# The gate's weights times `w_out`: summed on VectorE instead of multiplied on TensorE

## The chip, the cores and the metric

One NeuronCore of a Trainium2 chip. The metric is the device time of one launch in microseconds (us), as a median of runs. Engines are named as in the profile: PE is TensorE (matmuls; PEld are its weight loads), DVE is VectorE, ACT is ScalarE, POOL is GpSimd, SP is the engine whose queue issues most DMAs.

## What is computed

Sparse attention (4 batches, 8 heads, 576 positions, 64 wide), a gated mixture without routing, and a mixture of 8 experts with a greedy routing. Cut to what matters here:

```
x = attention(q, k, v)                   # 2304 tokens x 512
h = (x @ w1) * (x @ w2) @ w3             # 512 -> 1024 -> 1024
y = h @ w_out                            # 2304 x 512
logits = y @ w_gate                      # 2304 x 8
order = argsort(-logits)                 # greedy: each token one expert, 288 tokens per expert
out[mask_e] = relu(y[mask_e] @ e1[e]) @ e2[e]
```

`w_out` is 1024x512, `w_gate` 512x8, `w3` 1024x1024.

## The kernel before

The kernel never multiplies by `w3`, `w_out` and `w_gate` one after the other. It makes the product g = (x @ w1) * (x @ w2) for all tokens, and beside it two small weights: W = w3 @ w_out for the tokens' rows, and WG = w3 @ w_out @ w_gate for the logits, so that the routing can start from g @ WG at once.

Main products are exact to fp32 by splits: each operand is written as a high part h (rounded by ACT) and a rest l = x - h, and a product is h h + h l + l h (three fp32r matmuls). A split of a 128x1024 weight tile (`split`, L118 to L125) is one copy on ACT (L121) and one subtraction (L124): a single one of 1024 columns on DVE, or four of 256 columns on POOL where it is given `nc.gpsimd`.

The order of each engine's instructions is the order in which the Python program emits them. The mixture (`moe`, L445) is a generator that is run once for each batch b. For each f of 8 (128 columns of the 1024) it computes a = x @ w1 and b = x @ w2 into PSUM tiles of tag "ab" (four banks, used in turn), copies a to SBUF on ACT (L482) and multiplies it by b on DVE (L484: `g<-a,ps_ab`, or `gt<-a,ps_ab` for the 256-wide part). It yields before each step of matmuls: the 512-wide part has four steps of six matmuls for each f, the 256-wide part (b = 3 alone, the last 64 tokens of each batch together) two steps of twelve. The copy and the multiplication of a step are emitted at the yield behind it. The loop over batches puts other work between the steps: attention of later batches while b < 3, and for b = 3 the generator `gates` (L378), one piece a step.

`gates` makes WG. Before, in b = 3, from the fourth step on: eight turns, in which PE transposes four 128x128 blocks of `w_out` (L390, fetched as fp32 into the tiles `wo`) into PSUM, ACT copies them (L392, `wt`), and PE multiplies them by the gate's weights, padded to 32 columns (L398). The result is copied, transposed back (L411) and stands as the tile TS: for each of the 1024 rows of `w_out` its 8 products. Then TS times `w3` in two groups of 64 matmuls (L421), with six steps between them in which the second half of `w3` is loaded (`fetch_w3`), and two transposes (L433) give WG. Loads come from a DRAM scratch `kept`, on SP's queue. From the third f of the 512-wide part on, `place3` (L364) splits one pair of tiles of `w_out` and `w3` for the later product W, its subtraction on POOL.

The tile pools `p2` and `p3` (for `wo`, `wt`, `S`) take the room of the attention's pool `pa`, so their loads wait for attention's last instructions.

Of the kernel before, what the change touches and what calls it, by code (L numbers as in the profile page):

```python
# [32 lines left out]
C_I40, C_I96, C_PC = 136, 256, 352  # L33
C_PR, C_RS, C_M8, C_END = 460, 468, 612, 620

START, ATT_RATE, RUSH, LATE, EARLY, FIRST, ALONE = 8, 0.65, 0.65, 3, 7, 0.7, 18

ONE, GATHER_F = 2, 1

# [48 lines left out]
def body(tc, qk_d, v_d, ke_d, ve_d, msk_d, cst_d, tri_d, w1_d, w2_d, w3_d, wo_d, wg_d, e1_d, e2_d, out):  # L88
# [26 lines left out]
    def wtile(tag):  # L115

        return [wp.tile([128, 1024], F32R, tag=tag, name=tag + n, bufs=8) for n in "hl"]
# [243 lines left out]
        nc.sync.dma_start(t, kept[x])  # L361
        narrowed[x] = t

    def place3():  # L364
        n, i = to_split[placed[0]]
        k, tag = (2, "wa") if n == "wo" else (8, "wb")
        pre[n, i] = [x.rearrange("p (k n) -> p k n", k=k) for x in split(narrowed.pop((n, i)), *wtile(tag), nc.gpsimd)]
        placed[0] += 1
        if n == "w3" and i >= 2 and i + 2 < 8:
            fetch(("w3", i + 2), pm.tile([128, 1024], F32, tag="f", name="f", bufs=2))  # L370
# [4 lines left out]
    TS = TS[:, 256:].rearrange("p (m e) -> p m e", m=8)  # L375

    def gates():
        wg32 = p3.tile([128, 4, 32], F32, name="wg32", bufs=1)  # L378
        dve.memset(wg32, 0.0)
        dve.tensor_copy(wg32[:, :, 0:8], wg)  # L380
        dve.memset(TS, 0.0)
        acc = bank([128, 2, 128], "rt")

        def turn(r):
            g, i = divmod(r, 4)
            t = bank([128, 4, 128], "h")
            for q in range(4):
                w = narrowed["wo", 2 * g + q // 2]
                n0 = 512 * (q % 2) + 128 * i
                nc.tensor.transpose(t[:, q, :], w[:, n0:n0 + 128], ident)  # L390
            wt = p3.tile([128, 4, 128], F32, tag="wt", name="wt", bufs=2)
            act(wt, t, AF.Copy)  # L392
            return wt

        def gate(r, wt):
            g, i = divmod(r, 4)
            for q in range(4):
                mm(acc[32 * q:32 * q + 32, g, :], wg32[:, i, :], wt[:, q, :], start=(i == 0), stop=(i == 3))  # L398

        for r in range(0, 8, 2):  # L400
            wts = [turn(r), turn(r + 1)]
            yield
            yield
            for i in range(2):
                gate(r + i, wts[i])
        ts = p3.tile([128, 4, 128], F32, tag="wt", name="ts", bufs=2)[:, :2]
        act(ts, acc, AF.Copy)
        yield
        t = bank([128, 2, 128], "tr")
        for g in range(2):  # L410
            nc.tensor.transpose(t[:, g, :], ts[:, g, :], ident)  # L411
        dve.tensor_copy(TS.rearrange("p (g q) e -> p g q e", g=2)[:, :, :, 0:8],
                        t.rearrange("p g (q e) -> p g q e", q=4)[:, :, :, 0:8])
        yield

        acc = bank([128, 2, 128], "rt")
        for a, ms in enumerate(((4, 5, 6, 7), (0, 1, 2, 3))):
            ws = [narrowed["w3", m] for m in ms]
            for k in range(8):
                for q, w in enumerate(ws):  # L420
                    mm(acc[32 * q:32 * q + 32, a, :], TS[:, k, :], w[:, 128 * k:128 * k + 128],  # L421
                       start=(k == 0), stop=(k == 7))
            yield
            if ms[0]:
                fetch_w3(0)
                for _ in range(6):
                    yield
        wt = p3.tile([128, 4, 128], F32, tag="wt", name="wt", bufs=2)[:, :2]
        act(wt, acc, AF.Copy)
        yield  # L430
        t = bank([128, 2, 128], "tr")
        for a in range(2):
            nc.tensor.transpose(t[:, a, :], wt[:, a, :], ident)  # L433
        for a in range(2):
            dve.tensor_copy(WG[:, 4 - 4 * a:8 - 4 * a, :], t[:, a, :].rearrange("p (q e) -> p q e", q=4))

    def fetch_w3(m):
        x = p3.tile([128, 2, 1024], F32, tag="S", name="S", bufs=1)
# [7 lines left out]
    def moe(b):  # L446

        full = [(f, 2) for f in range(CUT[b] if b < 3 else 0, 8)]
        if b < 3:
            todo = [(f, h) for h in range(2) for f in range(CUT[b])] + full  # L450
        else:
            todo = [(f, 3) for f in range(8)] + full
        late = []
        for f, part in todo:
            if part == 3:
                xh, xl = XT
                if not GT:
                    GT.append(slot(0, [128, 8, 64 * B], F32, "gt"))
                ts, out = slice(0, 64 * B), GT[0][:, f]
            else:  # L460
                xh, xl = X[b]
                if b not in G:
                    G[b] = [slot(((4, 5), (6, 7), (8, 9), (1, 10))[b][i], [128, 4, MAIN], F32, "g") for i in range(2)]
                ts = (slice(0, HEAD), slice(HEAD, MAIN), slice(0, MAIN))[part]
                out = G[b][f // 4][:, f % 4, ts]
            nt = ts.stop - ts.start
            for n in (1, 2):
                for k in range(4):
                    if k == 0 or k == 2 and part == 2:
                        yield part, f, n  # L470
                        while late:
                            late.pop()()
                    if k == 0:
                        a = bank([128, nt], "ab")
                        wh, wl = W[n, f // 2]
                        fs = slice((f % 2) * 128, (f % 2) * 128 + 128)
                    mm(a, wh[:, k, fs], xh[:, k, ts], start=(k == 0), stop=False)  # L477
                    mm(a, wh[:, k, fs], xl[:, k, ts], start=False, stop=False)  # L478
                    mm(a, wl[:, k, fs], xh[:, k, ts], start=False, stop=(k == 3))  # L479
                if n == 1:  # L480
                    a_sb = pm.tile([128, MAIN], F32, tag="a", name="a", bufs=1)[:, :nt]
                    late.append(lambda x=a_sb, a=a: act(x, a, AF.Copy))  # L482
                else:
                    late.append(lambda x=a_sb, a=a, out=out: dve.tensor_tensor(out, x, a, op=OP.mult))  # L484
        while late:
            late.pop()()
# [21 lines left out]
        GS[c] = h, l  # L508


    wg = cst.tile([128, 4, 8], F32, name="wg")
    att = attention()
    qk_load(0)
# [17 lines left out]
            next(narrow, None)  # L531

    for b in range(B):
        if b == 3:
            stacks.pop("pa").close()
            p2 = pool("p2")
            p3 = pool("p3")
            for i in range(2):
                x = p2.tile([128, 2, 1024], F32, tag=f"P{i}", name="wo", bufs=1)
                for n in range(2):  # L540
                    fetch(("wo", 2 * i + n), x[:, n])
            fetch_w3(4)
            making_wg = gates()
        if b == 2:
            for _ in narrow:
                pass
        steps = 0
        for done, (part, f, n) in enumerate(moe(b)):
            if b == 0:
                while (n, f // 2) not in W:  # L550
                    next(narrow, None)
            while b < 3 and nxt is not None and nxt < NB * (b + 2) and (
                    steps < done * (RUSH if b == 0 else ATT_RATE) + (min(done, 8) * FIRST if b == 0 else 0) or nxt < NB * b + (8 if part else 4)):
                nxt = next(att, None)
                steps += 1
            if b < 2:
                next(narrow, None)
            if b == 3:
                if done >= LATE:
                    next(making_wg, None)  # L560
                while part == 2 and placed[0] // 2 < f // 2:
                    place3()
        while nxt is not None and nxt < NB * (b + 1) + (8 if b < 2 else 9):
            nxt = next(att, None)
    for _ in making_wg:
        pass
    while placed[0] < 8:
        place3()
# [14 lines left out]
    def make_w():  # L583

        for m in range(8):
            a = bank([128, D], "ab")
            for k in range(8):
                while ("wo", k // 2) not in pre or ("w3", m) not in pre:
                    place3()
                h, l = pre["w3", m]  # L590
                oh, ol = pre["wo", k // 2]
                mm(a, h[:, k, :], oh[:, k % 2, :], start=(k == 0), stop=False)
                mm(a, h[:, k, :], ol[:, k % 2, :], start=False, stop=False)
                mm(a, l[:, k, :], oh[:, k % 2, :], start=False, stop=(k == 7))
                yield 680
            evac(m, a)
            if placed[0] < 12:
                place3()
            if m in (4, 5):
                gsplit(m - 4)  # L600
        est.extend(pm.tile([128, 1024], F32, tag="f", name="est", bufs=2) for _ in range(2))
# [620 lines left out]
```

## Time and profile before

| | |
|---|---|
| median of 3 runs | 724.92 us (723.85 to 726.5) |
| the profiled execution | 727.11 us |
| its span, first to last instruction | 725.3 us |
| PE busy | 701.6 us, 97% of the span |
| DVE busy | 410.7 us, 57% |
| ACT busy | 353.2 us, 49% |
| POOL busy | 265.7 us, 37% |
| mean granted clock of PE | 0.978 of full speed |

Attention and the first three batches of the mixture fill about the first 223 us of the span, the last batch 223 to 301, then come the logits, W, the rows for the experts beside the routing, and the experts. Busy shares are means over stages with different limits. Matmuls are pipelined, so a row's duration is longer than the distance to the next row; it is the distance that counts.

### The profile page before, as it was taken

Reading aid. Unit: us, or ns where it says so; the run is one execution under the profiler, and the core shown is the slowest. Engines: PE = TensorE matmul, PEld = TensorE weight load, DVE = VectorE, ACT = ScalarE, POOL = GpSimd, SP = SyncE. Lnnn points to the kernel's source line nnn. Section 1 sums busy time; section 2 is a strip of 40 time slices with the busy share of each in tenths; the row PEclk is TensorE's granted clock in tenths of the full one; section 3 lists DMA queues with packets and bytes.
Section 4 is the critical chain, followed back from the end, with each engine's and each line's share of the span. In section 5 each row is a group of like instructions: output and inputs, shape, how many; then the busy total and the mean of one; then the engine's idle time right before and its main releaser. Section 6 shows DMA issues by size and latency. Waiting matters only on the chain.

```text
span 725.3 us, 15966 instructions
## 1 busy us (share of the span) xinstructions
PE 701.6 (97%) x6081; PEld 611.1 (84%) x6081; DVE 410.7 (57%) x1414; ACT 353.2 (49%) x812; POOL 265.7 (37%) x305
## 2 busy tenths in 40 slices
PE   4799999999999999999999999999999999999996
PEld 3689778888889988687877777799999999999995
DVE  5879867684312111167886768778888763234321
ACT  6666544454522222243445375447575656655432
POOL 2848512231100024533365353331414236655421
PEclk9589999999999999999999999999999999999998
DMA  8994687872105120110699999969988898996311
GB/s 302 340 280 165 219 331 271 298 271 104 52 5 228 39 79 1 60 35 31 117 131 136 169 137 232 155 205 225 248 239 244 197 277 226 299 288 188 93 33 33
DMA packets 59596, 126.66 MB, mean 175 GB/s; under 512 B 13696, under 2 KB 29440, under 8 KB 56960
## 3 DMA queue, kind: packets, MB, share of 16 engines
q1 hardware_dynamic: 27232, 89.46, 36.1%
q0 software_dynamic: 29696, 31.46, 26.3%
q10 hardware_dynamic: 2592, 4.72, 1.9%
q8 instruction: 48, 0.79, 0.4%
q14 instruction: 28, 0.23, 0.1%
HBM read 87.87 MB, written 15.73 MB: 143 GB/s over the span
## 4 chain that ended last, share of the span: by engine, by line
PE 84%; issue 6%; DVE 3%; POOL 2%; DMA 2%; ACT 1%; POOLq 0%; SPq 0%; ACTq 0%
PE ps_ab L477 10%; PE ps_ab L478 9%; PE ps_ab L479 9%; PE ps_ab L623 5%; PE ps_ab L625 4%; PE ps_ab L624 4%; PE ps_h L1047 4%; PE ps_h L1048 3%; PE ps_h L1049 3%; PE ps_ab L1071 3%; PE ps_ab L1072 3%; PE ps_ab L1073 3%; PE ps_rt L822 3%; PE ps_rt L228 2%; DMA qk<-qk_dram 2%
## 5 line engine op out<-in xcount | busy, mean ns | idle before, releaser
L207 POOL TENSOR_TENSOR p<-p,sm 128x384 f32<-128x384 f32 x36 | 45.8, 1283 | 123.0 <-DVE sm L205 75.4
L1071 PE MATMUL ps_ab<-hh,w 128*128 128x288 f32 x248 | 76.2, 307 | 0.0
L1073 PE MATMUL ps_ab<-hh,w 128*128 128x288 f32 x248 | 73.1, 295 | 0.0
L1072 PE MATMUL ps_ab<-hl,w 128*128 128x288 f32 x248 | 73.0, 294 | 0.0
L507 POOL DMA_DIRECT2D wbl<-g x36 | 48.4, 1675 | 61.1 <-ACT wbl L505 52.0
L1060 DVE SCALAR_TENSOR_TENSOR hl<-ps_h,hh 128x288 fp32r<-128x288 f32 x62 | 28.2, 455 | 70.3 <-ACT hh L1059 70.1
L1059 ACT ACTIVATE hh<-ps_h 128x288 fp32r<-128x288 f32 x62 | 25.5, 412 | 84.0 <-PE ps_h L1049 81.3
L200 ACT ACTIVATE p<-p,sm 128x96 f32<-128x96 f32 x144 | 52.0, 363 | 25.2 <-DVE sm L193 24.3
L482 ACT ACTIVATE a<-ps_ab 128x512 f32<-128x512 f32 (+1 forms) x44 | 22.9, 522 | 81.4 <-PE ps_ab L479 73.0
L623 PE MATMUL ps_ab<-Wx,wbh 128*128 128x512 f32 x144 | 59.6, 414 | 0.0
L625 PE MATMUL ps_ab<-Wx,wbl 128*128 128x512 f32 x144 | 56.2, 391 | 0.0
L477 PE MATMUL ps_ab<-x,wah 128*128 128x512 f32 (+1 forms) x144 | 55.5, 386 | 0.7 <-ACT x L251 0.7
L624 PE MATMUL ps_ab<-Wx,wbh 128*128 128x512 f32 x144 | 56.2, 390 | 0.0
L477 PE MATMUL ps_ab<-x,wbh 128*128 128x512 f32 (+1 forms) x144 | 54.5, 379 | 0.0
L478 PE MATMUL ps_ab<-x,wah 128*128 128x512 f32 (+1 forms) x144 | 54.0, 375 | 0.0
L479 PE MATMUL ps_ab<-x,wal 128*128 128x512 f32 (+1 forms) x144 | 53.7, 373 | 0.0
L479 PE MATMUL ps_ab<-x,wbl 128*128 128x512 f32 (+1 forms) x144 | 53.3, 370 | 0.0
L478 PE MATMUL ps_ab<-x,wbh 128*128 128x512 f32 (+1 forms) x144 | 53.2, 370 | 0.0
L484 DVE TENSOR_TENSOR g<-a,ps_ab 128x512 f32<-128x512 f32 (+1 forms) x36 | 22.5, 624 | 54.0 <-PE ps_ab L479 51.1
L1072 PEld LDWEIGHTS ps_ab<-hl,w 128*128 128x128 f32 x248 | 46.7, 188 | 0.1
L1071 PEld LDWEIGHTS ps_ab<-hh,w 128*128 128x128 f32 x248 | 46.7, 188 | 0.0
L1073 PEld LDWEIGHTS ps_ab<-hh,w 128*128 128x128 f32 x248 | 46.5, 188 | 0.0
(296 smaller groups left out, 2044.3 us busy)
## 6 DMA issues: line engine op xcount, KB each, us to landing
est<-e_dram SPq DMA_DIRECT2D x53, 512.0 KB, 5.9
w<-w_dram SPq DMA_DIRECT2D x16, 1024.0 KB, 8.0
qk<-qk_dram SPq DMA_DIRECT2D x36, 320.0 KB, 4.7
w<-est POOLq DMA_DIRECT2D x20, 512.0 KB, 7.8
wbl<-g POOLq DMA_DIRECT2D x28, 256.0 KB, 6.5
v<-v_dram SPq DMA_DIRECT2D x36, 192.0 KB, 4.4
kept<-f SPq DMA_DIRECT2D x12, 512.0 KB, 4.1
rows<-e_dram SPq DMA_DIRECT2D x11, 512.0 KB, 5.8
```

Source lines behind the costliest of these rows:

```text
L200: act(p[:, i, :], p[:, i, :], AF.Exp, bias=sm[:, 1, i:i + 1], scale=-1.0, accum_out=sm[:, 2, i:i + 1])
L207: nc.gpsimd.tensor_tensor(p, p, sm[:, 3, :, None].to_broadcast([128, 4, KB]), op=OP.mult)
L477: mm(a, wh[:, k, fs], xh[:, k, ts], start=(k == 0), stop=False)
L478: mm(a, wh[:, k, fs], xl[:, k, ts], start=False, stop=False)
L479: mm(a, wl[:, k, fs], xh[:, k, ts], start=False, stop=(k == 3))
L507: nc.gpsimd.dma_start(x, src, accum_op=OP.add)
L623: mm(a, h[:, f, :], wh, start=(f == 0), stop=False)
L624: mm(a, h[:, f, :], wl, start=False, stop=False)
L625: mm(a, l[:, f, :], wh, start=False, stop=(f == 7))
L1071: mm(y, wh[:, f % 2, ds_], h, start=(f == 0), stop=False)
L1072: mm(y, wh[:, f % 2, ds_], l, start=False, stop=False)
L1073: mm(y, wl[:, f % 2, ds_], h, start=False, stop=(f == end))
```

## The change

TS is no longer made by PE. The gate's weights (128 x 32) are transposed once on PE (L380 of the changed kernel), copied by ACT (`ws`) and written to DRAM as `wgt`, 32 rows of 128. For each of the 8 experts SP reads its 512 weights back, replicated over all 128 partitions (`wt`, two buffers). DVE then multiplies each of the eight 128x512 blocks of `w_out` by that row and sums along the row, one column of TS an instruction (L400): 64 instructions, two a mixture step, all with the same unused full output `waste`. The generator starts as soon as attention's last instructions are emitted, within b = 2, and is stepped within `moe`, behind the late copies and products. The `w3` loads stand behind `wgt` and the first two rows. Splits start when WG is done; those up to the eighth are now on DVE, the others stay on POOL.

```
-    def place3():
+    def place3(eng=None):
...
-        pre[n, i] = [x.rearrange("p (k n) -> p k n", k=k) for x in split(narrowed.pop((n, i)), *wtile(tag), nc.gpsimd)]
+        pre[n, i] = [x.rearrange("p (k n) -> p k n", k=k) for x in split(narrowed.pop((n, i)), *wtile(tag), eng)]
...
     def gates():
...
-        for r in range(0, 8, 2):
-            wts = [turn(r), turn(r + 1)]
+
+        t = bank([32, 128], "h")
+        nc.tensor.transpose(t, wg.rearrange("p c e -> p (c e)"), ident)
+        ws = p3.tile([32, 128], F32, name="ws", bufs=1)
+        act(ws, t, AF.Copy)
+        wgt = dram.tile([32, 128], F32, name="wgt")
+        nc.sync.dma_start(wgt, ws)
         dve.memset(TS, 0.0)
+        waste = p3.tile([128, 512], F32, name="waste", bufs=1)
+
+        def row(e):
+            w = p3.tile([128, 4, 128], F32, tag="wt", name="wt", bufs=2)
+            nc.sync.dma_start(w, wgt.rearrange("(c e) p -> e c p", c=4)[e:e + 1].to_broadcast([128, 4, 128]))
+            return w.rearrange("p c n -> p (c n)")
+
+        rows = [row(e) for e in range(2)]
+        fetch_w3(4)
+        for _ in range(3):
             yield
+        for e in range(8):
+            w = rows.pop(0)
+            for m in range(8):
+                dve.tensor_tensor_reduce(waste, narrowed["wo", m // 2][:, 512 * (m % 2):512 * (m % 2) + 512], w, scale=1.0,
+                                         scalar=0.0, op0=OP.mult, op1=OP.add, accum_out=TS[:, m, e:e + 1])
+                if m % 2:
+                    yield
+            if e < 6:
+                rows.append(row(e + 2))
...
                         while late:
                             late.pop()()
+                        for x in side:
+                            next(x, None)
...
+            if b == 2 and nxt is not None and nxt >= NT:
+                nxt = None
+                stacks.pop("pa").close()
...
+                side.append(gates())
             if b == 3:
-                if done >= LATE:
-                    next(making_wg, None)
-                while part == 2 and placed[0] // 2 < f // 2:
+                if gated and part == 2 and placed[0] < 6:
                     place3()
...
-                    place3()
+                    place3(nc.gpsimd)
```

How the order moves. On PE in the 256-wide part of b = 3, before, a gate product and the next transposes stand between two steps of the mixture:

```order
L479 MATMUL ps_ab<-xt,wal 128x256
L398 MATMUL ps_rt<-wt,wg_2891 32x128 x8
L390 MATMUL ps_h<-C,wo 128x128 x8
L477 MATMUL ps_ab<-xt,wbh 128x256
L478 MATMUL ps_ab<-xt,wbh 128x256
```

In the changed kernel nothing stands there, and the first group of TS times `w3` (now L412) comes in the 512-wide part, half way through the second product of its fourth f:

```order
L471 MATMUL ps_ab<-x,wbh 128x512
L472 MATMUL ps_ab<-x,wbh 128x512
L473 MATMUL ps_ab<-x,wbl 128x512
L412 MATMUL ps_rt<-S,TS 32x128 x2
L412 MATMUL ps_rt<-f,TS 32x128 x2
```

That group reads TS, so PE's queue stands there until DVE has made all of TS. On DVE at the end of b = 2 and the start of b = 3, before, with the semaphores that each row waits for in brackets:

```order
L484 TENSOR_TENSOR g<-a,ps_ab 128x512 [waits PE_49]
L484 TENSOR_TENSOR g<-a,ps_ab 128x512 [waits PE_49,Activation_49]
L484 TENSOR_TENSOR gt<-a,ps_ab 128x256 [waits PE_49,Activation_49]
L379 MEMSET wg_2891 128x128 [waits DMAHW4_49,DMAHW3_49,DMAHW5_49,DMAHW2_49,DMAHW6_49,DMAHW1_49,DMAHW7_49,DMAHW0_49,Pool_49]
L380 COPY wg_2891<-wg 128x4x8 [waits DVE_49]
```

And in the changed kernel, where a sum is two rows, the sum itself and the read of its accumulator into TS:

```order
L478 TENSOR_TENSOR g<-a,ps_ab 128x512 [waits PE_49]
L385 MEMSET TS 128x256
L400 ISA waste,TS<-wo,wt 128x512 [waits DMAHW3_49,DMAHW4_49,DMAHW2_49,DMAHW5_49,DMAHW1_49,DMAHW6_49,DMAHW0_49,DMAHW7_49,DVE_49,Pool_49]
L400 ISA TS 128x1
L400 ISA waste,TS<-wo,wt 128x512 [waits DVE_49]
L400 ISA TS 128x1
L478 TENSOR_TENSOR g<-a,ps_ab 128x512 [waits PE_49,Activation_49]
L400 ISA waste,TS<-wo,wt 128x512 [waits DMAHW6_49,DVE_49]
L400 ISA TS 128x1
L400 ISA waste,TS<-wo,wt 128x512 [waits DVE_49]
```

The last product of b = 2 now stands behind the first two sums, and each sum carries a wait for DVE's own semaphore, DVE_49. On SP, behind the loads of `wo`, before:

```order
L361 DMA wo<-kept 128x1024 x3
L361 DMA S<-kept 128x1024 x2
L361 DMA f<-kept 128x1024 x2
```

and in the changed kernel:

```order
L361 DMA wo<-kept 128x1024 x3
L384 DMA wgt<-ws 32x128 [waits Activation_49]
L390 DMA wt<-wgt 128x4x128 [waits DMAHW1_49]
L390 DMA wt<-wgt 128x4x128
L361 DMA S<-kept 128x1024
```

The read of the first row waits for a DMA's semaphore, and the loads of `w3` (into `S` and `f`) stand behind it.

## Rows read from the trace of the kernel before

**Rows 1.** The page, part 1: busy us (share of the span) xinstructions.

```profile
PE 701.6 (97%) x6081; PEld 611.1 (84%) x6081; DVE 410.7 (57%) x1414; ACT 353.2 (49%) x812; POOL 265.7 (37%) x305
```

**Rows 2.** The page, part 4: the chain that ended last, by engine.

```profile
PE 84%; issue 6%; DVE 3%; POOL 2%; DMA 2%; ACT 1%; POOLq 0%; SPq 0%; ACTq 0%
```

**Rows 3.** Stretch table: us, busy us (instructions) by engine, clock, DMA share, GB/s.

```profile
216.00:301.00 85.00, 85.00 (x653) 73.67 (x653) 11.91 (x28) 21.47 (x39) 18.06 (x26) 1.00 0.22 81
```

**Rows 4.** Timeline of PE, 227 to 301: start, us, line, operation, tiles, shapes, count.

```profile
227.40 1.04 PE L390 MATMUL ps_h<-C,wo 128*128 128x128 f32 x8
228.19 0.36 PE L477 MATMUL ps_ab<-xt,wbh 128*128 128x256 f32 x1
...
231.23 0.65 PE L398 MATMUL ps_rt<-wt,wg 128*32 128x128 f32 x16
...
232.65 0.36 PE L477 MATMUL ps_ab<-xt,wbh 128*128 128x256 f32 x1
...
244.63 0.65 PE L398 MATMUL ps_rt<-wt,wg 128*32 128x128 f32 x16
245.20 0.39 PE L477 MATMUL ps_ab<-xt,wbh 128*128 128x256 f32 x1
...
246.73 0.38 PE L411 MATMUL ps_tr<-C,ts 128*128 128x128 f32 x2
246.87 0.36 PE L477 MATMUL ps_ab<-xt,wah 128*128 128x256 f32 x1
...
300.78 1.50 PE L891 MATMUL ps_h<-g,TS 128*32 128x512 f32 x12
```

**Rows 5.** The chain in order of time: the first group of TS times `w3`.

```profile
248.55 1.88 PE ps_rt L421 x64
```

**Rows 6.** Timeline of DVE: a product of the mixture, [idle before, releaser].

```profile
279.20 0.69 DVE L484 TENSOR_TENSOR g<-a,ps_ab 128x512 f32<-128x512 f32 x1 [4.75 <-PE ps_ab L479]
```

**Rows 7.** Timeline of DVE: two multiply-and-sums of attention in a row.

```profile
190.94 0.25 DVE L193 CUSTOM_DVE_ANT_0 p<-ps_h,msk 128x96 f32<-128x96 f32 x1
191.12 0.08 DVE L193 DVE_READ_ACCUMULATOR2_ANT sm<- 128x1 f32 x1
191.12 0.25 DVE L193 CUSTOM_DVE_ANT_0 p<-ps_h,msk 128x96 f32<-128x96 f32 x1
```

**Rows 8.** Groups of DVE by line: xcount | busy us, mean ns | idle before.

```profile
L193 DVE CUSTOM_DVE_ANT_0 p<-ps_h,msk 128x96 f32<-128x96 f32 x116 | 22.7, 251 | 0.1
L967 DVE TENSOR_TENSOR wal<-est,wah 128x256 fp32r<-128x256 f32 x40 | 14.3, 418 | 0.0
L124 DVE TENSOR_TENSOR w<-est,w 128x1024 fp32r<-128x1024 f32 x6 | 7.4, 1225 | 2.9 <-ACT w L121 2.9
L866 DVE CUSTOM_DVE_ANT_0 r_sm<-r_r,C 128x8 f32<-128x8 f32 x7 | 1.2, 171 | 0.2
```

**Rows 9.** Timeline of DVE: a reduction of the routing and an instruction that waits for it.

```profile
325.10 0.26 DVE L824 TENSOR_SCALAR_CACHE_REDUCE r_tj<-ps_rt,r_rp 128x40 bf16<-128x40 f32 x1 [0.70 <-PE ps_rt L822]
325.28 0.08 DVE L824 DVE_READ_ACCUMULATOR r_tj<-ps_rt,r_rp 128x1 f32 x1
325.40 0.21 DVE L825 STREAM_TRANSPOSE r_jt<-r_jp 128x32 f32<-128x32 f32 x1
```

**Rows 10.** Timeline of ACT: attention's last copy.

```profile
217.65 0.39 ACT L252 ACTIVATE xt<-ps_rt 128x128 fp32r<-128x128 f32 x1
```

**Rows 11.** The tile `wo`: its loads on SP's queue, and their time to landing.

```profile
L361 SPq DMA_DIRECT2D wo<-kept x4: 345/429/433, 216.4 to 217.7; - x4
...
DMA to landing us min/median/max: 3.2/4.9/6.5
```

**Rows 12.** DMA issues of 216 to 220: count, KB each, median us to landing.

```profile
f<-kept SPq DMA_DIRECT2D x2, 512.0 KB, 9.2
```

**Rows 13.** DMA issues of 170 to 172, with nothing in the queue ahead.

```profile
v<-v_dram SPq DMA_DIRECT2D x2, 192.0 KB, 2.5
```

**Rows 14.** The page, part 6: DMA issues of the whole span.

```profile
wbl<-g POOLq DMA_DIRECT2D x28, 256.0 KB, 6.5
```

**Rows 15.** Stretch table, columns as in rows 3: a pause of PE and what follows.

```profile
102.00:106.00 4.00, 2.44 (x54) 1.94 (x53) 2.04 (x10) 2.89 (x14) 1.42 (x1) 0.98 0.76 260
106.00:109.00 3.00, 3.00 (x7) 2.15 (x8) 2.90 (x16) 1.55 (x9) 0.61 (x1) 0.50 0.95 365
```

More of the change, by code (lines that the diff above doesn't have):

```diff
@@ L34 @@
 C_PR, C_RS, C_M8, C_END = 460, 468, 612, 620
-START, ATT_RATE, RUSH, LATE, EARLY, FIRST, ALONE = 8, 0.65, 0.65, 3, 7, 0.7, 18
+START, ATT_RATE, RUSH, EARLY, FIRST, ALONE = 8, 0.65, 0.65, 7, 0.7, 18
 ONE, GATHER_F = 2, 1
@@ L377, in gates @@
     def gates():
-        wg32 = p3.tile([128, 4, 32], F32, name="wg32", bufs=1)
-        dve.memset(wg32, 0.0)
-        dve.tensor_copy(wg32[:, :, 0:8], wg)
-        dve.memset(TS, 0.0)
[L382 to L398, printed above, removed]
-        for r in range(0, 8, 2):
-            wts = [turn(r), turn(r + 1)]
-            yield
[L403 to L414, printed above, removed]
+        t = bank([32, 128], "h")
+        nc.tensor.transpose(t, wg.rearrange("p c e -> p (c e)"), ident)
+        ws = p3.tile([32, 128], F32, name="ws", bufs=1)
+        act(ws, t, AF.Copy)
@@ L435, in gates @@
             dve.tensor_copy(WG[:, 4 - 4 * a:8 - 4 * a, :], t[:, a, :].rearrange("p (q e) -> p q e", q=4))
+        gated.append(True)
     def fetch_w3(m):
@@ L508, in gsplit @@
         GS[c] = h, l
+    side, gated = [], []
     wg = cst.tile([128, 4, 8], F32, name="wg")
@@ L533, in body @@
     for b in range(B):
[L534 to L543, printed above, removed]
         if b == 2:
@@ L557, in body @@
                 next(narrow, None)
+            if b == 2 and nxt is not None and nxt >= NT:
+                nxt = None
+                stacks.pop("pa").close()
+                p2 = pool("p2")
+                p3 = pool("p3")
+                for i in range(2):
+                    x = p2.tile([128, 2, 1024], F32, tag=f"P{i}", name="wo", bufs=1)
+                    for n in range(2):
+                        fetch(("wo", 2 * i + n), x[:, n])
+                side.append(gates())
             if b == 3:
-                if done >= LATE:
-                    next(making_wg, None)
-                while part == 2 and placed[0] // 2 < f // 2:
+                if gated and part == 2 and placed[0] < 6:
                     place3()
@@ L564, in body @@
             nxt = next(att, None)
-    for _ in making_wg:
+    assert nxt is None
+    for _ in side[0]:
         pass
@@ L597, in make_w @@
             if placed[0] < 12:
-                place3()
+                place3(nc.gpsimd)
             if m in (4, 5):
```

## The prediction

> **What bounds the kernel now.** I read the page's shares first: TensorE (PE) is busy for 97% of the span and VectorE (DVE) for 57% [rows 1], and PE carries 84% of the chain that ended last [rows 2]. So a microsecond of matmuls that goes is a microsecond gained, as long as nobody else becomes late. Then I read the stretch that is changed, 216 to 301 us, as a table by engine: PE is busy for all 85.0 us at full clock (1.00, the 2.4 GHz level), DVE for 11.9 of them, GpSimd for 18.1 [rows 3]. It looks as if DVE could take a lot of work here for nothing. The reader should hold on to the second thought: in this stretch PE never waits, so whoever is late for PE by 1 us costs the whole 1 us.
>
> **What PE loses.** In the timeline of PE the gate's work lies between the matmuls of the mixture, and its price is the distance from its start to the next mixture matmul [rows 4]. The first eight transposes (L390) run from 227.40 to 228.19, 0.79 us. A gate product and the next eight transposes (L398, L390) run from 231.23 to 232.65, 1.42 us, and there are three of these. The last product takes 244.63 to 245.20, 0.57 us, and the two transposes back (L411) 246.73 to 246.87, 0.14 us. Together 0.79 + 3 x 1.42 + 0.57 + 0.14 = 5.8 us. One transpose of the gate's weights (L380 of the changed kernel) comes in; two cost 0.14 us, and it pays for its own switch, so I take 0.2 us. Net: **PE's own work is 5.6 us shorter.** The product with w3 (L421, 1.88 us a group [rows 5]) stays, but comes later: its first group now stands in the fourth of the eight 512-wide f of the mixture, half way through the second product.
>
> **When PE would get there.** A step is what lies between two yields of the mixture. Two steps of the 256-wide part take 231.23 - 228.19 = 3.04 us [rows 4]; a 512-wide f takes 4.75 + 0.69 = 5.44 us from one product on DVE to the next, so 1.36 us for each of its four steps [rows 6]. Mixture work ends at 300.78 [rows 4]. Counting back from 300.78 - 5.6 = 295.2 the 17 steps that follow the first group (23.1 us), the two groups (3.8 us) and the transposes back (0.14 us), PE would be ready for that group at 268.2, were it never held.
>
> **What DVE gets.** 64 multiply-and-sums of 128x512. The same kind of instruction is there now (L193, 128x96): 0.25 us long, and started every 0.18 us, because the next one starts before it ends [rows 7]. The plain two-operand forms grow by (1225 - 418) / (1024 - 256) = 1.05 ns a column [rows 8], which makes 251 + 416 x 1.05 = 0.69 us for 512; the two shapes of the same instruction, 128x8 at 171 ns and 128x96 at 251 ns, would make 0.63 us, the lower bound. I take 0.69, since a plain multiply of 128x512 is also 0.69 [rows 6].
>
> How far apart they start matters more. L193 writes a new slice each time and waits for nothing of its own engine. The 64 new ones all write the same tile, `waste`, and in the order each waits for DVE's own semaphore, that is, for the end of the one before. The nearest rows with such a wait are L824 to L825: a reduction of 0.26 us, its accumulator read, and the next starts 0.30 us after the first [rows 9]; so length plus 0.04 us, 0.73 us here. Without the wait it would be the length less 0.08, 0.61 us. I take 0.73.
> The Trainium skill speaks against this: "VectorE: DVE Perf Modes", section "The DRAIN you can't avoid", says that a chain with a semaphore after each operation takes as long as one without. By that rule the 64 would stand 0.61 us apart, which is the first rival below. The trace does not agree: 0.08 us of overlap without a wait [rows 7], 0.04 us of gap with one [rows 9].
>
> Among the 64 stand 12 products of the mixture (eight 128x256, four 128x512; the order shows them). An instruction in front of one needs no wait, so: 52 x 0.73 + 12 x 0.61 = 45.3 us, and the 12 products 8 x 0.34 + 4 x 0.61 = 5.2 us, their lengths of 0.42 and 0.69 less the same 0.08 [rows 6, 8]. **From the first to the last sum DVE needs 50.4 us.** The 32 mixture steps beside it take PE 16 x 1.52 + 16 x 1.36 = 46.1 us, so DVE cannot catch up.
>
> **When DVE can start.** It needs the first replicated row of the gate's weights. ScalarE is free at 218.04 [rows 10]; a copy of 0.3 us puts `ws` there at 218.4. SP issues the four `wo` loads from 216.4 to 217.7; the first lands after 3.2 us, the last after 6.5, at 224.2 [rows 11], and the loads behind them take 9.2 us [rows 12]: they go one after the other. The write of `wgt` stands behind `wo` and lands at 224.3; only then may SP issue the first replicated read. Nothing in the trace reads one row 128 times. The nearest are 192 KB in 2.5 us with nothing ahead [rows 13] and a 256 KB transfer of GpSimd's in 6.5 us [rows 14]. I take 3.2 us, near the first (same queue, nothing ahead): **DVE starts at 227.6**, with bounds from 224.0 (if the small write isn't held behind `wo`) to 231.0.
>
> **The sum.** DVE ends at 227.6 + 50.4 = 278.0; PE was ready at 268.2 and waits 9.8 us in all: part of it earlier, because the product behind the first sums is held and with it the fourth accumulator bank, the rest at the four-row product. Minus 5.6, plus 9.8: 4.2 us. Such a pause has a second price. From 102 to 106 us PE was busy for 2.44 of 4 us, and from 106 to 109 the granted clock stood at 0.50 (the 1.2 GHz level), though PE was busy throughout [rows 15]: some 3.3 us at half speed, 1.7 us lost. After a pause of several us I expect the same once: 1.7 us, with bounds 0 and 3.3. **Total: +5.9 us.**
> The other edits cost nothing. Eight splits go from GpSimd to DVE (the order shows eight, six in the loop and two behind it): 8 x 1.23 us on DVE [rows 8]. All stand behind the sums, where DVE is nearly idle; the last is needed in the product of `w3` and `wo`, behind the logits. If this cover were gone, two splits, 2.5 us, would show. The first `w3` loads are now issued behind `wgt` at about 225 and land by 235, at the 9.2 us of [rows 12], long before 278. The second `w3` loads are issued when the first group is done and used seven steps later, as now; a load that came late there would show as a wait at the second group. The other six replicated rows must each land within DVE's 6.3 us for eight sums in the 256-wide part; at 3.2 us they do.
> Against the profiled execution (727.11, span 725.3) this gives 733.0. The median of the runs is 724.92, 2.2 us lower, so the forecast for it is **730.8 us**.
>
> **Rivals.**
> 1. *The wait on its own engine costs nothing.* Then the sums stand 0.61 us apart, 64 x 0.61 + 5.2 = 44.2 us, DVE ends at 271.8 and PE waits 3.6 us, in two pieces; I leave the clock as it is. -5.6 + 3.6 = -2.0: 722.9, not slower. It decides below 0.64 us a sum: then DVE ends before 268.2 + 5.6 = 273.8 and gain and wait are equal, (273.8 - 227.6 - 5.2) / 64. For it speaks the overlap of [rows 7], against it the gap of [rows 9]. Chance 0.13.
> 2. *DVE is never late*: rows at 221 already and 0.61 us a sum. Then the whole 5.6 us are gained, 719.3. Against: the loads queue up [rows 11, 12]. Chance 0.04.
> 3. *The replicated rows are slow.* From 5.9 us of landing on, DVE waits for each of the last six. At 7 us: a start of 231.4 (+3.8) and 6 x 1.1 = 6.6 more, 741.2. For: nothing in the trace reads one place 128 times; against: the 2.5 us of [rows 13]. Chance 0.11.
> The change might also not do what it says, if PE kept the transposes; the order shows them gone.
>
> **How the numbers follow.** The forecast has the rest, 0.72. Its own range goes from 725.5 (start at 224.0, clock unchanged: -5.6 + 6.2) to 735.8 (start at 231.0, half clock twice as long: -5.6 + 13.2 + 3.3). The range for 8 in 10 reaches from 725 to 738: it leaves out rivals 1 and 2 and the slower part of rival 3. A measurement here can tell about 0.5% (3.6 us) from no change. Faster by more, below 721.3: rival 2 and a little of rival 1, 0.07. Within 0.5%: most of rival 1 and the forecast's lower end (an early start, or a clock that stays), 0.23. Slower, above 728.5: 0.70.
>
> **What would show it.** In the changed profile: sums of 0.69 us that start 0.73 us apart; the first at about 227.6, behind a DMA; PE waiting for DVE at the four-row product (L412) for about 7 us, and about 2 us before it for an accumulator bank; a clock of 0.50 for some us behind that; logits that start at about 306.5 instead of 300.8, and the same time from there to the end. It is wrong if sums start 0.61 us apart, if PE's wait at L412 is under 3 us, or if the difference arises behind the logits.

## The result and the profile after

The changed kernel takes 732.7 us as a median of 6 runs (731.53 to 736.73), beside it the kernel before 724.42 us (723.83 to 727.74): ratio 1.0114, 95% interval 1.0082 to 1.0147. Run again later, beside other runs of the kernel before, it was 1.0132 (1.0115 to 1.0149). So the change costs some 8 to 9.5 us; forecast were 5.9. The profiled execution took 734.78 us, its span is 733.0.

The page of the changed kernel, part 1 (busy us, share of the span, instructions) and the chain that ended last, by engine:

```profile
PE 698.5 (95%) x5984; PEld 606.9 (83%) x5984; DVE 461.4 (63%) x1547; ACT 349.1 (48%) x804; POOL 243.5 (33%) x273
...
PE 73%; issue 9%; DVE 9%; DMA 3%; POOL 2%; ACT 1%; SPq 0%; POOLq 0%; DVEq 0%; ACTq 0%
```

PE has 3 us less to do than in [rows 1] and the kernel is longer all the same: in the chain DVE has grown from 3% to 9% [rows 2], at PE's expense. Where PE waited, by the view of waits, from 216 to 301 us (line and tile, what it waited for: us, times, longest):

```profile
PE ps_ab L471 <- DVE g L478: 6.1, 1, 6.1
PE ps_rt L412 <- DVE TS L400: 1.7, 4, 0.8
PE ps_rt L412 <- issue: 1.3, 1, 1.3
```

In the kernel before this list is empty. The first line is an accumulator bank held by a product of the mixture, the other two are the four-row product (TS times `w3`). Their places in the timeline of PE:

```profile
221.26 0.28 PE L471 MATMUL ps_ab<-xt,wah 128*128 128x256 f32 x1
...
225.46 0.28 PE L473 MATMUL ps_ab<-xt,wal 128*128 128x256 f32 x1
231.86 0.58 PE L471 MATMUL ps_ab<-xt,wbh 128*128 128x256 f32 x1 [6.13 <-DVE g L478]
...
273.08 0.39 PE L473 MATMUL ps_ab<-x,wbl 128*128 128x512 f32 x1
274.80 0.30 PE L412 MATMUL ps_rt<-S,TS 128*32 128x128 f32 x2 [1.33 <-issue]
...
275.49 0.30 PE L412 MATMUL ps_rt<-S,TS 128*32 128x128 f32 x2 [0.26 <-DVE TS L400]
...
278.17 0.43 PE L412 MATMUL ps_rt<-S,TS 128*32 128x128 f32 x2 [0.31 <-DVE TS L400]
...
280.96 0.80 PE L471 MATMUL ps_ab<-x,wbh 128*128 128x512 f32 x1
...
308.42 1.06 PE L885 MATMUL ps_h<-g,TS 128*32 128x512 f32 x8
```

The first row is the first 256-wide matmul of b = 3, the last one the start of the logits. The distance between the two is called **the stretch** below, and it is the best measure of the change, since attention ahead of it scatters by some us from run to run: 87.15 us here, 77.69 in the kernel before (to 300.78 [rows 4], from the row below), so 9.46 us more.

```profile
223.09 0.28 PE L477 MATMUL ps_ab<-xt,wah 128*128 128x256 f32 x1
```

From the logits to the first expert it is 180.55 us here and 180.52 before, and from there to the end 244.0 in both: nothing arises behind the logits.

The section on the change says that PE stands at the four-row product until all of TS is made; the rows show otherwise. The product starts at 274.80, and its pieces come one by one as the last expert's eight sums do, of which the last starts at 279.62 (below). The mixture goes on at 280.96, 0.65 us behind the end of that sum. PE works between the pieces, so the view of waits counts only 3.0 us in this place.

DVE in the same places (the read of its accumulator is an instruction of its own):

```profile
217.31 0.27 DVE L385 MEMSET TS<- 128x256 f32 x1
229.77 0.69 DVE L400 CUSTOM_DVE_ANT_0 waste<-wo,wt 128x512 f32<-128x512 f32 x1 [12.20 <-issue]
...
235.60 0.69 DVE L400 CUSTOM_DVE_ANT_0 waste<-wo,wt 128x512 f32<-128x512 f32 x1
236.22 0.08 DVE L400 DVE_READ_ACCUMULATOR2_ANT TS<- 128x1 f32 x1
236.34 0.69 DVE L400 CUSTOM_DVE_ANT_0 waste<-wo,wt 128x512 f32<-128x512 f32 x1
...
240.22 0.69 DVE L400 CUSTOM_DVE_ANT_0 waste<-wo,wt 128x512 f32<-128x512 f32 x1
...
240.84 0.42 DVE L478 TENSOR_TENSOR gt<-a,ps_ab 128x256 f32<-128x256 f32 x1
241.17 0.69 DVE L400 CUSTOM_DVE_ANT_0 waste<-wo,wt 128x512 f32<-128x512 f32 x1
...
279.62 0.69 DVE L400 CUSTOM_DVE_ANT_0 waste<-wo,wt 128x512 f32<-128x512 f32 x1
```

Sums start 0.74 us apart here, 0.73 on average; ahead of a product, which does not wait, it is 0.62. DVE idles 12.2 us ahead of the first one. Its row names no releaser; the view of the tile `wgt` does, under those who waited for it (us, times):

```profile
  DVE waste L400: 12.2, 1
```

How long the way through DRAM took stands in SP's timeline:

```profile
214.41 1.77 SPq L361 DMA_DIRECT2D wo<-kept  x4
216.35 0.42 SPq L384 DMA_DIRECT2D wgt<-ws  x1
223.28 0.93 SPq L390 DMA_DIRECT2D wt<-wgt  x2
```

and in the DMA issues (count, KB each, median us to landing):

```profile
wgt<-ws SPq DMA_DIRECT2D x1, 16.0 KB, 6.9
...
wt<-wgt SPq DMA_DIRECT2D x2, 256.0 KB, 7.6
```

The 16 KB of `wgt` take 6.9 us behind the `wo` loads; the first row is issued at 223.28, and the first sum starts 6.5 us later. And the clock, from the stretch table (columns as in [rows 3]):

```profile
226.00:232.00 6.00, 0.14 (x1) 0.14 (x1) 2.19 (x6) 0.10 (x1) 0.00 (x0) 0.84 0.61 193
232.00:237.00 5.00, 5.00 (x24) 5.00 (x25) 4.83 (x15) 0.67 (x2) 0.00 (x0) 0.51 0.65 260
...
278.00:284.70 6.70, 6.29 (x41) 3.81 (x42) 2.90 (x9) 0.00 (x0) 0.00 (x0) 0.50 0.41 142
```

PE works at the 1.2 GHz level (0.50) for 5 us behind the first wait, and for 6.7 us from the middle of the four-row product on.

The 9.46 us are made up thus. At full clock a 256-wide matmul comes every 0.12 us, a 512-wide one every 0.228 and a group of the four-row product takes 1.88. The pause behind 225.46 costs 6.40 - 0.12 = 6.3 us. The 24 matmuls from 231.86 on take 5.2 instead of 2.9 us: 2.3. From 273.08 to 280.96 it is 7.88 instead of 0.23 + 1.88: 5.8, the 3.0 us of the view and the slow pace of the pieces. The ten matmuls from 280.96 on take 4.1 instead of 2.3: 1.8. Together 16.2, less what PE no longer does (6.55, by e7 below).

### The profile page after: what moved, and what is told of

Read it like the earlier page. It is cut to its first block, busy times and chain, and to the rows that moved or that the text cites. A ratio compares the mean times of both kernels' runs of the same rounds, so it can differ in the third digit from the quotient of the medians.

```text
span 733.0 us, 15876 instructions
## 1 busy us (share of the span) xinstructions
PE 698.5 (95%) x5984; PEld 606.9 (83%) x5984; DVE 461.4 (63%) x1547; ACT 349.1 (48%) x804; POOL 243.5 (33%) x273
## 4 chain that ended last, share of the span: by engine, by line
PE 73%; issue 9%; DVE 9%; DMA 3%; POOL 2%; ACT 1%; SPq 0%; POOLq 0%; DVEq 0%; ACTq 0%
PE ps_ab L471 7%; PE ps_ab L472 6%; PE ps_ab L473 6%; PE ps_ab L617 5%; PE ps_ab L618 4%; PE ps_ab L619 4%; DVE waste L400 4%; PE ps_h L1041 4%; PE ps_h L1042 3%; PE ps_h L1043 3%; PE ps_ab L1065 3%; PE ps_ab L1066 3%; PE ps_ab L1067 3%; PE ps_rt L816 3%; DMA qk<-qk_dram 2%
## 5 line engine op out<-in xcount | busy, mean ns | idle before, releaser
L400 DVE CUSTOM_DVE_ANT_0 waste<-wo,wt 128x512 f32<-128x512 f32 x64 | 44.2, 690 | 14.0 <-issue 12.2
```

What stands on the lines that cost most here:

```text
L400: dve.tensor_tensor_reduce(waste, narrowed["wo", m // 2][:, 512 * (m % 2):512 * (m % 2) + 512], w, scale=1.0, scalar=0.0, op0=OP.mult, op1 ...
```

## The experiments

Theory A is the prediction's: one chain, the first row's landing plus 64 sums at 0.73 us, sets the end of the four-row product, and PE's waits are what is left of it. Rival B: the pace belongs to the instruction, whatever it waits for. Rival C: the loss is the early pause itself. Each kernel was run beside the kernel before on its chip, so ratios compare; absolute times differ by some us from one group of runs to the next. Of the kernels, e5 alone has a single run and so no ratio.

| us | first sum behind the first 256-wide matmul | last sum ends behind it | stretch | ratio (95%) |
|---|---|---|---|---|
| before | | | 77.69 | 1 |
| changed | 8.5 | 59.1 | 87.15 | 1.0114 (1.0082 to 1.0147) |
| changed, again | 8.7 | 59.2 | 86.67 | 1.0132 (1.0115 to 1.0149) |
| e1 own slices | 8.3 | 52.6 | 78.77 | 1.0025 (1.0006 to 1.0043) |
| e2 rows first | 4.5 | 55.1 | 83.60 | 1.0087 (1.0058 to 1.0115) |
| e3 both | 4.9 | 49.3 | 75.38 | 0.9987 (0.9971 to 1.0003) |
| e4 product first | 7.5 | 57.6 | 85.86 | 1.0133 (1.0095 to 1.0171) |
| e5 w3 later | 8.5 | 59.1 | 87.27 | |
| e6 splits on GpSimd | 8.2 | 58.8 | 86.02 | 1.0144 (1.0125 to 1.0163) |
| e7 rows preloaded, own slices | 0.1 | 44.5 | 71.14 | 0.9926 (0.9914 to 0.9938) |
| e8 before, splits on DVE | | | 77.69 | 0.9999 (0.9984 to 1.0014) |
| e9 rows preloaded, one waste | -3.1 | 49.5 | 77.61 | 1.0015 (1.0004 to 1.0025) |

**e1, the pace.** The sums write four slices in turn:

```diff
-        waste = p3.tile([128, 512], F32, name="waste", bufs=1)
+        waste = slot(1, [128, 4, MAIN], F32, "waste")
-                dve.tensor_tensor_reduce(waste, ...
+                dve.tensor_tensor_reduce(waste[:, m % 4, :], ...
-                    G[b] = [slot(((4, 5), (6, 7), (8, 9), (1, 10))[b][i], ...
+                    G[b] = [slot(((4, 5), (6, 7), (8, 9), (10, 1))[b][i], ...
```

> The sums write four slices in turn instead of the one tile waste, so that a sum no longer waits for the one just before it (the slices lie in the room of a dead batch of x; one g tile of the last batch changes places with it). Theory A (VectorE's chain sets the end, and the wait on its own engine is 0.12 us of each of 52 sums): sums start 0.61 to 0.62 us apart instead of 0.735, the last ends 6.1 us earlier, at about 274.2 by the changed kernel's clock instead of 280.3; TensorE, which would come to the four-row product at 273.3, waits about 1 us there and keeps its clock, which saves 5.8 us of wait and 1.9 us of half clock: 725.1 us. Rival B (a sum and the read of its accumulator take 0.735 us whatever they wait for): 732.7, no change. The first sum and the pause of TensorE behind 225.5 stay as they are in both.

Its timeline of DVE:

```profile
236.37 0.69 DVE L400 CUSTOM_DVE_ANT_0 waste<-wo,wt 128x512 f32<-128x512 f32 x1
236.98 0.09 DVE L400 DVE_READ_ACCUMULATOR2_ANT TS<- 128x1 f32 x1
236.98 0.69 DVE L400 CUSTOM_DVE_ANT_0 waste<-wo,wt 128x512 f32<-128x512 f32 x1
```

and all that PE waits for from 214 to 320 us:

```profile
PE ps_ab L471 <- DVE g L478: 5.8, 1, 5.8
```

The next sum starts in the same moment as the read of the accumulator, 0.61 us behind the sum. From the first sum to the end of the last it is 44.3 us instead of 50.5, the waits at the four-row product are gone, and the stretch is 8.4 us shorter (7.7 were expected). B has fallen. The slices lie in other room than the one tile did; that the room alone changes nothing was not tried. The early pause stays, and with it 1.1 us more than before.

**e2 and e3, the start.** `wgt` is written at the start of b = 2, and the first two rows stand ahead of `wo` on SP; e3 has the slices of e1 too.

```diff
+    def turned_wg():
...
+        ws = ws_room[:32, :128]
...
         if b == 2:
...
+            turned_wg()
...
+                side.append(gates())
+                next(side[0])
                 for i in range(2):
                     x = p2.tile([128, 2, 1024], F32, tag=f"P{i}", name="wo", bufs=1)
...
-                side.append(gates())
```

> The gate's weights are transposed and written to DRAM at the start of b = 2, and SP reads the first two replicated rows ahead of the wo loads; waste stays one tile. Theory A: the first row lands about 5 us after SP may issue it, at 219, the first sum starts at about 220.5 instead of 229.8, the last ends at 271.0 instead of 280.3 with sums still 0.735 us apart; TensorE loses nothing behind 225.5 and waits about 6 us at the four-row product, whose half clock behind it stays: 9.3 us less, 723.4 us. Rival B gives the same here. Rival C (what costs is the early pause of TensorE alone, 6.3 us of bank wait and 2.3 us of half clock): 724.1, with little wait at the four-row product. Rival D (the start hangs on wo, not on the rows: first sum not before 224): 727 or more.

> Both edits, own slices for the sums and the rows first. Theory A: first sum at about 221.1, sums 0.61 us apart, the last ends at 265.5 while TensorE comes to the four-row product at 264.7: waits of under 1.5 us in all, no half clock. All the 16 us that TensorE lost to waits and half clock in the stretch are gone: 717.2 us, 1.0% faster than the kernel before. Rival B (0.735 us a sum whatever it waits for): as the kernel with the rows first, about 723.4. Rival C: 724.

Both were too hopeful about the start, and rival D of e2 was right: the first sum came 4.5 and 4.9 us behind the first 256-wide matmul, not at it. In e2 DVE's timeline has it so:

```profile
226.49 0.69 DVE L405 CUSTOM_DVE_ANT_0 waste<-wo,wt 128x512 f32<-128x512 f32 x1 [8.14 <-DMA wo<-kept]
```

and the DMA issues of 214 to 223 us:

```profile
wo<-kept SPq DMA_DIRECT2D x4, 512.0 KB, 10.8
...
wt<-wgt SPq DMA_DIRECT2D x2, 256.0 KB, 9.2
```

The wait has only changed its name: now `wo` stands behind the rows and needs 10.8 us instead of 4.9 [rows 11]. In e3 the first sum's row names a matmul of PE instead (8.55 us, L478); its start differs from e2's by 0.4 us, so it is put down to `wo` as well, which e3 alone does not show. The pace was 0.73 in e2, as in the changed kernel, and 0.61 in e3, as in e1.

e3's stretch is 2.3 us shorter than before, its ratio only 0.13% (0.9 us) below 1. The difference fits a wait ahead of the stretch: e2, e3, e7 and e9 transpose the gate's weights at the start of b = 2, and there PE waits 1.3 us for DVE (the second line of e9's waits below), where the kernel before and the changed one have no wait. With these 1.3 us added, e3 is 1.0 us faster by the stretch and 0.9 by the ratio, e7 5.25 and 5.4 faster, e9 1.2 and 1.1 slower, e2 7.2 and 6.3 slower. A kernel with that transpose alone moved was not run.

**e4, the early pause.** The last product of b = 2 goes ahead of the first sums.

```diff
-        for _ in range(3):
+        for _ in range(4):
             yield
...
-                if m % 2:
+                if m % 2 and (e, m) != (7, 5):
                     yield
```

> The last product of b = 2 stands ahead of the first two sums instead of behind them, by one more step before the first sum; the last four sums share a step, so that the four-row product stays where it is. Nothing of the sums' start or pace changes. Theory A: TensorE's pause behind 225.5 shrinks by one f of the 256-wide part, 2.9 us, and comes back at the four-row product, since VectorE's last sum ends only 0.6 us earlier (one product fewer among the sums): 732.1 us. Rival C (the pause behind 225.5 and its half clock are themselves the loss): 2.9 to 5.2 us less, 727.5 to 729.8.

```profile
PE ps_rt L412 <- issue: 3.7, 1, 3.7
PE ps_ab L471 <- DVE gt L478: 3.4, 1, 3.4
```

In these waits of PE the early pause has shrunk from 6.1 to 3.4 us, and the wait at the four-row product has grown, from 3.0 to 3.7 by the view and from 7.88 to 9.80 by the distance from the last mixture matmul ahead of it to the first behind it. The ratio, 1.0133, is that of the changed kernel, not the 1.004 to 1.007 of rival C (727.5 to 729.8 over 724.42), which has fallen: what PE saves at the start it waits for at the four-row product.

**e5, what the row waits for.** The first `w3` loads are issued behind the second expert's sums.

```diff
         rows = [row(e) for e in range(2)]
-        fetch_w3(4)
...
+            if e == 1:
+                fetch_w3(4)
```

> The changed kernel with the first four w3 loads issued behind the sums of the second expert instead of right behind the first two rows. If the w3 loads behind them slow the rows: the first row lands about 4.6 us after its issue, as the later rows do, and the first sum starts about 6.5 - 1.5 = 5 us behind the first row's issue instead of 6.5. If one row read 128 times takes that long by itself: 6.5 us again. The time follows the first sum, 1.5 us less or the same.

SP's timeline:

```profile
218.63 0.34 SPq L384 DMA_DIRECT2D wgt<-ws  x1
226.67 12.34 SPq L390 DMA_DIRECT2D wt<-wgt  x3
```

DVE's first sum:

```profile
232.09 0.69 DVE L399 CUSTOM_DVE_ANT_0 waste<-wo,wt 128x512 f32<-128x512 f32 x1 [12.23 <-issue]
```

and the DMA issues of 226 to 229 us:

```profile
wt<-wgt SPq DMA_DIRECT2D x2, 256.0 KB, 5.2
```

From the issue to the first sum it is 5.4 us instead of 6.5: the loads behind the rows cost them about 1 us, and with none behind them the two rows land in 5.2 (median) instead of 7.6. The write of `wgt` took 8.0 us in this run, so that the sums began no earlier.

**e6 and e8, the splits.** e6 is the changed kernel with its first eight splits on GpSimd, e8 the kernel before with those of the loop on DVE.

```diff
-                    place3()
+                    place3(nc.gpsimd)
...
     while placed[0] < 8:
-        place3()
+        place3(nc.gpsimd)
```

```diff
-    def place3():
+    def place3(eng=nc.gpsimd):
...
-                    place3()
+                    place3(None)
```

> The changed kernel with its first eight splits back on GpSimd, the sums as they are. By the prediction the move of the splits costs and gains nothing, as they stand behind the sums and are not needed before the product of w3 and wo: the same time as the changed kernel, ratio to the kernel before 1.011, within 0.3%. Rival: VectorE's splits delay its products or the logits' work: 2.5 us or more faster than the changed kernel, ratio under 1.008; or GpSimd's slower splits are late for the product of w3 and wo: ratio over 1.015.

> The kernel before with only its splits inside the mixture's loop on VectorE instead of GpSimd, no sums. By the prediction: the same time, ratio 1.000 within 0.3%. Rival (a split of 1.23 us in front of a product on VectorE holds TensorE's accumulator bank): slower by 1 us or more.

e6's ratio, 1.0144, lies within the intervals of the changed kernel; e8's is 0.9999, and its stretch that of the kernel before to the hundredth. Where the splits run costs nothing that can be measured.

**e7, start and pace together.** On top of e3, rows 0 to 3 are read during b = 2 into the two tiles `f`, which are idle then; `wo` is first in the queue again.

```diff
+    def rows_in_f():
+        for j in range(2):
+            x = pm.tile([128, 1024], F32, tag="f", name="f", bufs=2).rearrange("p (e c n) -> p e c n", e=2, c=4)
+            first.extend(row_to(x[:, i], 2 * j + i) for i in range(2))
...
-        rows = [row(e) for e in range(2)]
+        rows = list(first)
         yield
-        fetch_w3(4)
+        rows.extend(row(e) for e in (4, 5))
+        x = p3.tile([128, 2, 1024], F32, tag="S", name="S", bufs=1)
+        for i in range(2):
+            fetch(("w3", 4 + i), x[:, i])
...
+            if e in (1, 3):
+                fetch(("w3", 6 + e // 2), pm.tile([128, 1024], F32, tag="f", name="f", bufs=2))
-            if e < 6:
+            if e in (4, 5):
                 rows.append(row(e + 2))
...
+            if b == 2 and done == 8:
+                rows_in_f()
```

> As the kernel with own slices and rows first, but no row is loaded at attention's end: the gate's weights are written at the start of b = 2, and the rows of four experts are read then, into the two tiles f that stand idle until w3 comes; wo is first in SP's queue again, rows 4 and 5 behind it, and the two w3 loads into f follow when their rows are used up. Theory A (the sums' start was bound by what SP's queue carried at attention's end, first the rows, then wo; the pace is 0.61 us with own slices): first sum right behind TensorE's last matmul of b = 2, where the slices of waste come free, so about at the first 256-wide matmul instead of 5 us behind it; the last sum ends 44.4 us later, about 1 us behind TensorE's arrival at the four-row product; no pause over 1 us, no half clock; from the first 256-wide matmul to the logits 71 to 72 us instead of 77.7 in the kernel before, so 6 us faster than the kernel before: ratio 0.992. Rival E (a sum at 0.61 us slows TensorE or its feeding copies in some other way, or the early sums hold products of the mixture): 74 us or more in that stretch, ratio 0.996 or more.

Its DMA issues of 168 to 176 us:

```profile
f<-wgt SPq DMA_DIRECT2D x4, 256.0 KB, 5.9
...
wgt<-TS SPq DMA_DIRECT2D x1, 16.0 KB, 2.8
```

DVE's first sum:

```profile
224.61 0.69 DVE L417 CUSTOM_DVE_ANT_0 waste<-wo,f 128x512 f32<-128x512 f32 x1 [3.70 <-DMA wo<-kept]
```

and the stretch table from 224 to 296 us:

```profile
224.00:296.00 72.00, 72.00 (x522) 62.86 (x524) 54.53 (x153) 15.33 (x25) 0.34 (x3) 1.00 0.24 80
```

PE is busy without a gap at full clock, while DVE works for 54.53 of 72 us beside it. The row of the first sum names the load of `wo`, but e9 below starts 3.1 us ahead of the first 256-wide matmul with the same loads; so what held e7's sums until that matmul was likely the room of the slices, which b = 2 still reads. The stretch is 71.14 us, 6.55 less than before, and the ratio 0.9926: **faster than both kernels**, 719.77 us against 725.29 for the kernel before beside it.

**e9, the start alone.** e7 with the one tile `waste`, and the `g` tiles where the changed kernel has them.

```diff
-        waste = slot(1, [128, 4, MAIN], F32, "waste")
+        waste = p3.tile([128, 512], F32, name="waste", bufs=1)
...
-                dve.tensor_tensor_reduce(waste[:, m % 4, :], ...
+                dve.tensor_tensor_reduce(waste, ...
-                    G[b] = [slot(((4, 5), (6, 7), (8, 9), (10, 1))[b][i], ...
+                    G[b] = [slot(((4, 5), (6, 7), (8, 9), (1, 10))[b][i], ...
```

> The kernel with the preloaded rows, but all sums write the one tile waste again, and the g tiles of the last batch stand as in the changed kernel. It gives the worth of the early start alone. Theory A (start and pace add up along one chain that ends at the four-row product): first sum between 1.5 us ahead of the first 256-wide matmul and at it, sums 0.735 us apart, the last ends 49 to 50.5 us behind it, TensorE is there 43.4 us behind it: it waits 5 to 6 us there, and its clock falls once behind that. No pause at the first products. From the first 256-wide matmul to the logits 71.1 + 5.5 + 1.9 = 78.5 us (77.7 in the kernel before, 87.2 in the changed one): ratio to the kernel before 1.001. Rival B (a late start was all that was wrong, the pace is hidden): 71 to 73 us, ratio 0.993.

Its waits of PE from 160 to 310 us:

```profile
PE ps_rt L431 <- DVE TS L417: 1.7, 4, 0.8
PE ps_h L382 <- DVE sm L193: 1.3, 1, 1.3
PE ps_rt L431 <- issue: 0.3, 1, 0.3
```

and the clock behind them, in the stretch table:

```profile
268.00:272.00 4.00, 3.46 (x41) 1.42 (x42) 2.73 (x8) 0.00 (x0) 0.00 (x0) 0.56 0.02 4
```

The first and the third are at the four-row product, where the clock falls; the second is at the moved transpose of the gate's weights, outside the stretch. The time is that of the kernel before to 0.15%. From the 87.15 us of the changed kernel the pace alone takes off 8.4 (e1), the start alone 9.5 (e9), both together 16.0 (e7): that is less than the 17.9 of the two, since in e7 DVE is not late any more, and since its sums start 3.2 us later than e9's.

**The changed kernel again**, unaltered, beside e9.

> The changed kernel again, unaltered, beside the others: 87 us from the first 256-wide matmul to the logits, ratio to the kernel before 1.011 to 1.014.

It gave 86.67 us and a ratio of 1.0132, so e6 and e4 are to be held against 1.011 to 1.013.

## Why the prediction was right, and where it was off

The direction, the mechanism and the chain were right, and the time lies inside the range. The median moved by 8.3 us where 5.9 were forecast. Point by point:

- **PE's own work, -5.6 us.** e7, with no pause and full clock, gives 71.14 - 77.69 = -6.55. The term was 0.9 too small. In the trace before, the matmuls at the edges of the removed pieces stand 0.20 to 0.23 us from the next instead of 0.12: ahead of the four gate products (231.02 to 231.23) and behind the six pieces (228.19 to 228.40), ten edges or some 0.9 us, which the distances taken did not hold. The 0.2 taken for the new transpose falls outside the stretch as well, as that runs at 215.70. Nor would PE have come to the four-row product at 268.2, 45.1 us behind the first 256-wide matmul, but 43.6 behind it (e7).
- **The pace, 0.73 us a sum and 50.4 us in all.** Measured 0.73 and 50.5, and 0.61 once the wait on the own engine is gone (e1). The choice between [rows 7] and [rows 9] decided the forecast, and rival 1 went with it. The Trainium skill ("VectorE: DVE Perf Modes", section "The DRAIN you can't avoid") would have given no difference between the two; the runs differ by 0.12 us an instruction, 8.4 us of the stretch.
- **The start, 227.6: this step failed.** By the kernel before it was 4.5 us behind the first 256-wide matmul; measured 8.5, past the upper bound (231.0, or 7.9). The write of `wgt` landed 0.8 us later than taken, the first row needed 6.5 us from its issue to the sum instead of 3.3. I had put the row near the 2.5 us of [rows 13]; it was near the 6.5 us of [rows 14]. By e5 some 5.2 of that are the row's own and about 1 the loads behind it. That the small write is held behind `wo` was right: 6.9 us there, 2.8 alone (e7).
- **The two waits, about 2 and 7 us.** Measured 6.3 and 5.8 by distance. The prediction called itself wrong with a wait of under 3 us at L412; by the view of waits it is 3.0 (2.9 in the repeat), on that border, since the product follows the sums piece by piece and was taken to wait as a whole. The start that came 4.0 us later went to the first one, as it must: the product behind the first sums holds the bank until they run. By e4 it makes no difference in which of the two PE waits.
- **The clock, 1.7 us once.** It fell twice, 2.3 and 1.8 us. The first fall cost nothing of its own: PE was at the four-row product at 273.3, DVE's last sum ended at 280.3, and PE would have waited for that time there.
- **The sum.** -6.55 + 6.3 + 2.3 + 5.8 + 1.8 = 9.65, measured 9.46. Along the chain: the start 4.0 us later than forecast, the sums 0.1 longer, and from the end of the last sum to the logits 28.1 us instead of 28.7, together 3.5 more than the 5.9. The 733.0 of the forecast is the time of the profiled execution, which was 734.78; that its span is 733.0 means nothing. The span grew by 7.7 us and not by 9.46 by luck: attention ahead of the stretch was 1.8 us shorter in that execution.
- **Splits at no cost, `w3` loads in time, nothing behind the logits**: right (e6, e8, the waits, the 180.5 us).
- **Rivals 2 and 3.** Rival 2 is what e7 makes true: 0.61 us a sum and rows in time give the whole gain in the stretch. Of rival 3 the first row was slow, but the six later rows of the changed kernel landed in 4.8 us (median), under the 5.9 from which DVE would wait for each.

## What to carry to other kernels

When work moves from the busiest engine to an idle one, cost the chain that feeds the idle one first: here 64 cheap sums were late by a wait that a spare tile removes, and by a small write and a read that stood in a full queue. A dead output that all instructions share is still a dependency; give it a few places in turn. Data that is ready long before belongs in room that is idle earlier: putting the load first in the crowded queue only moved the wait to the next load (e2), reading it 40 us earlier removed it (e7).

## What the runs showed of the hardware

A row of 2 KB read 128 times (256 KB) took 5.2 us with no `w3` loads behind it (e5) and 7.6 in front of them (changed kernel), where an ordinary 192 KB took 2.5 [rows 13]. A 16 KB write took 2.8 us with no loads just ahead of it (e7) and 6.3 to 8.0 behind 2 MB of loads (e4, e5). An accumulating instruction of 128x512 starts 0.73 us behind the one before when it waits for it, and 0.61 when it does not (e1), even though DVE does nothing else in between. And the clock: with early pauses of PE of 2.4 and 2.7 us, from one matmul to the next (e2, e3), the granted clock stayed at 1.00 (the 2.4 GHz level); with those of 3.7 (e4), 6.1 (e1) and 6.4 us (changed kernel) it fell to 0.50 (1.2 GHz). The length of one pause does not settle it: at the four-row product, where PE follows DVE's sums, it fell to 0.50 in e2 and e9 too, where no single wait was over 1.9 and 0.8 us, and stayed at 1.00 in e3, where none was over 0.2. In e2, the early pause from 226 to 228.6 and what followed:

```profile
226.00:228.00 2.00, 0.45 (x4) 0.24 (x3) 1.47 (x5) 0.00 (x0) 0.00 (x0) 1.00 1.02 418
...
230.00:232.00 2.00, 1.98 (x17) 1.78 (x16) 1.97 (x6) 0.23 (x1) 0.00 (x0) 1.00 0.79 320
```
